# Decay rows in a tile of two units and a tile of four, first weights behind the third chunk's loads: one change to a chunked scan with a feed-forward block

## The chip, the cores and the metric

The kernel runs on one core of one Trainium2 chip. The metric is device microseconds of one execution, from launch to the last store. The kernel before takes 327.71 us, the median of three runs (324.82 to 328.68).

## The reference, cut to what matters

Two stages follow each other. The first is a scan with decay over 768 positions for 4 batches and 8 heads (head width 32, state width 16), done in chunks. The second is a feed-forward block of width 2048 over the 3072 resulting tokens of width 256.

```python
log_a = np.log(np.clip(a, 1e-06, 1.0))
for c in range(nc):                                   # chunk after chunk
    cum = np.cumsum(la, axis=-1)                      # la: this chunk of log_a
    L = np.exp(cum[:, :, :, None] - cum[:, :, None, :]) * causal
    CB = np.einsum('bhin,bhjn->bhij', Cc, Bc)         # scores
    y_intra = np.einsum('bhij,bhjd->bhid', CB * L, xc)
    y_inter = np.einsum('bhin,bhnd->bhid', Cc, state) * np.exp(cum)[:, :, :, None]
    y[:, :, sl] = y_intra + y_inter
    state = decay_full[:, :, None, None] * state + np.sum(Bx, axis=2)
...
h = x @ w_in                                          # x: y as (tokens, 256)
g = np.maximum(0.01 * h, h)
return (g @ w_out).astype(np.float32)
```

## The kernel before, in words

**Units.** A chunk is 96 positions, so there are 8 chunks of 4 batches: 32 units, each with all 8 heads of one batch in one chunk. Unit u belongs to chunk u // 4. For every unit the kernel needs a decay tile `lt` (the exponentials L for the 8 heads, with the decay to the carried state appended), multiplies scores into it and contracts the result with x.

**Two ways to a decay tile.** Units 0 and 1 get theirs from masks alone (`decay_direct`). Units 2 to 15 get theirs from TensorE (`decay_pe`, L245): one product of a left tile `dl` and a right tile `dr` makes the differences of the cumulative sums in PSUM tile `pd`, and ScalarE takes the exponential (L261). The constant rows of `dl` and `dr` are filled once (`fill_pair`, `fill_less`). The rows that depend on the unit come from `parts_d`, the cumulative sums split in three bf16 parts and stored to HBM, by two loads (`decay_rows_of`, L238 into `dr` and L241 into `dl`). Before, there are two `dl`/`dr` pairs with two units each; when the two units of a pair have been used by TensorE, the next two units' rows are loaded into it. Units 16 to 31 take another way (`decay_rows`, `decay_sub`, `decay_exp`: a broadcast load, a subtraction on GpSimd and an exponential), worked off in pairs by `pair_block` between the steps of the feed-forward block.

**The lead.** The loop over u from 0 to 14 (L616) does the first 16 units one after the other. In its round u stand, in this order: the scores of unit u + 1 (TensorE L305, VectorE L310), the decay of unit v = u + 2 (L248, L261), the products of unit u (L322, and L331 for the state to carry), ScalarE's copies out (L353, L358), then loads on the SyncE queue: rows for later decay tiles, `bc` (B and C), `bn` (B again, for the state), `xs` (x) and `raw` (the coded weights of one block f of the hidden width). The state of a unit goes through GpSimd (L356) into the x tile of the same batch one chunk later. `LEAD_PASSES` says in which rounds one or more decode passes run.

**Decoding weights.** Each of the 16 blocks f of the weights comes as 64-bit numbers in two halves and is decoded to a high part `wh` and a low part `wl` of fp32 by five passes on VectorE (hold L412, shift L418, sign L425, low L432, rest L445) and two on ScalarE (`decode_abs` L407 ahead of the five, `decode_high` L438 ahead of rest). `RAWS` is the number of raw tiles; the load of block f + RAWS is issued when the low pass of block f is done.

**The feed-forward block.** 96 steps (t, f): a token tile t of 512 and a block f. Step s runs six matmuls into `hp` (L508: x high with w high, x high with w low, x low with w high, for two halves), an activation on ScalarE, the low half of it on VectorE (L521), and three steps later six matmuls of the second product (L536). The steps start with t = 0, 1, 2 in turn for the first 7 blocks f, and go on with f = 7 to 15 for t = 0, then 1, then 2, and then t = 3, 4, 5. `PAIR` names the step at which the block of each pair of later units stands; its loads, subtraction and exponential stand five, three and two steps ahead. When the last f of a token tile is through, `take` adds the parts (L559) and stores. `late_sums`, at the end of step 24, makes the cumulative sums for units 16 to 31.

The order on every engine is the order in which the program is written: each engine works through its own queue and waits on semaphores. SyncE runs ahead of the others until one of its loads waits for a free buffer.

## Time and profile before

| what | value |
|---|---|
| time, median of three runs | 327.71 us (324.82 to 328.68) |
| the profiled execution's own time | 328.9 us |
| its span, first to last instruction | 327.2 us |
| mean granted TensorE clock | 0.982 |
| TensorE matmul busy | 317.5 us, 97% |
| ScalarE busy | 168.1 us, 51% |
| VectorE busy | 161.0 us, 49% |
| GpSimd busy | 78.0 us, 24% |
| moved by DMA | 27.86 MB |
| first feed-forward matmul starts | 41.02 us |

In the profile PE is TensorE's matmul, PEld its weight load, DVE VectorE, ACT ScalarE, POOL GpSimd and SPq the queue of loads and stores on SyncE. A row of a timeline is: start in us, length in us, engine, line of the kernel, operation, output and inputs with sizes, count, and in brackets the idle time before it with what ended it. The chain of waits is followed back from the last instruction. A row of the table of stretches gives the stretch, its length, the busy time of each engine with the count of instructions, then the granted TensorE clock (1.00 is full speed), the mean busy share of the DMA engines and the rate in GB/s. The profiled execution took 328.9 us, 1.2 us above the median of the timed runs and 1.7 us longer than its own span.

### The profile page before, as it was taken

How to read it: one execution, taken by the hardware profiler on the slowest of the kernel's cores; microseconds unless marked ns; L12 is line 12 of the kernel's file. 1: busy time of each engine (PE TensorE's matmuls, PEld its weight loads, DVE VectorE, ACT ScalarE, POOL GpSimd, SP SyncE). 2: the span in 40 equal slices, each digit the busy share in tenths (PEclk: the TensorE clock that was granted, in tenths of full speed). 3: DMA queues.
4: the chain of work that ended last, by engine and by line, in shares of the span. 5: the costliest groups of instructions: out<-in, count | busy, mean ns of one | idle time of the engine just before them, and what ended most of it. 6: DMA issues, size and time to landing. Idle time of an engine off the chain costs nothing.

```text
span 327.2 us, 6238 instructions
## 1 busy us (share of the span) xinstructions
PE 317.5 (97%) x2425; PEld 251.6 (77%) x2425; DVE 161.0 (49%) x308; ACT 168.1 (51%) x335; POOL 78.0 (24%) x164
## 2 busy tenths in 40 slices
PE   8969999999999999999999999999999999999994
PEld 4546688888887887788688878888878788888883
DVE  7637989888888524352615352425252212322221
ACT  5645768566667353535354535454544433433331
POOL 4735740000000133335434235252410000000000
PEclk9967999999999999999999999999999999999999
DMA  5795413333350560120263054302010000100001
GB/s 174 219 271 182 137 66 128 128 128 130 92 191 0 156 180 0 66 86 0 103 200 86 1 172 132 86 0 87 2 64 0 2 0 2 62 4 0 2 0 65
DMA packets 11527, 27.86 MB, mean 85 GB/s; under 512 B 2313, under 2 KB 2793, under 8 KB 11497
## 3 DMA queue, kind: packets, MB, share of 16 engines
q1 hardware_dynamic: 11353, 27.33, 26.5%
q8 instruction: 19, 0.31, 0.4%
q10 hardware_dynamic: 144, 0.13, 0.1%
q14 instruction: 11, 0.09, 0.1%
HBM read 24.14 MB, written 3.32 MB: 84 GB/s over the span
## 4 chain that ended last, share of the span: by engine, by line
PE 94%; DMA 2%; ACT 1%; DVE 1%; issue 1%; SPq 0%; ACTq 0%; DVEq 0%
PE hp L508 39%; PE py L536 35%; PE sc L536 5%; PE sc L305 2%; PE sc L382 2%; DMA dl<-parts_d 2%; PE sc L322 2%; PE py L322 2%; PE pd L248 2%; PE sc L508 1%; PE sc L109 1%; PE py L331 1%; DVE lt L310 0%; PE sc L331 0%; PE pd L225 0%
## 5 line engine op out<-in xcount | busy, mean ns | idle before, releaser
L521 DVE TENSOR_TENSOR gl<-hp,gh 128x512 fp32r<-128x512 f32 x94 | 65.0, 692 | 141.6 <-ACT hp L518 141.6
L515 ACT ACTIVATE gh<-hp 128x512 fp32r<-128x512 f32 x94 | 56.3, 599 | 111.3 <-PE hp L508 111.2
L508 PE MATMUL hp<-xh,wh 128*128 128x512 f32 x188 | 73.4, 390 | 0.0
L508 PE MATMUL hp<-xl,wh 128*128 128x512 f32 x188 | 73.2, 389 | 0.0
L508 PE MATMUL hp<-xh,wl 128*128 128x512 f32 x188 | 73.1, 389 | 0.0
L536 PE MATMUL py<-gh,wh 128*128 128x512 f32 x164 | 65.3, 398 | 0.7 <-ACT gh L515 0.7
L536 PE MATMUL py<-gh,wl 128*128 128x512 f32 x164 | 63.9, 390 | 0.0
L536 PE MATMUL py<-gl,wh 128*128 128x512 f32 x164 | 63.9, 389 | 0.0
L518 ACT ACTIVATE hp<-hp 128x512 f32<-128x512 f32 x94 | 55.7, 593 | 0.0
L508 PEld LDWEIGHTS hp<-xl,wh 128*128 128x128 f32 x188 | 35.3, 188 | 7.4
L508 PEld LDWEIGHTS hp<-xh,wh 128*128 128x128 f32 x188 | 35.3, 188 | 7.4
L508 PEld LDWEIGHTS hp<-xh,wl 128*128 128x128 f32 x188 | 35.3, 188 | 7.3
L271 POOL TENSOR_TENSOR lt<-lt,ccol 112x768 f32<-112x768 f32 x16 | 23.5, 1470 | 69.8 <-DMA lt<-crow_d 68.1
L356 POOL COPY xs<-stage 16x64 f32<-16x64 f32 x112 | 28.4, 254 | 45.7 <-ACT stage L353 25.6
L536 PEld LDWEIGHTS py<-gh,wh 128*128 128x128 f32 x164 | 30.8, 188 | 9.9 <-issue 2.0
L536 PEld LDWEIGHTS py<-gl,wh 128*128 128x128 f32 x164 | 30.8, 188 | 6.5
L536 PEld LDWEIGHTS py<-gh,wl 128*128 128x128 f32 x164 | 30.8, 188 | 6.0
L280 POOL TENSOR_SCALAR_AFFINE_SELECT lt<-lt 96x768 f32<-96x768 f32 x16 | 14.0, 877 | 41.0 <-ACT lt L279 41.0
L310 DVE TENSOR_TENSOR lt<-sc,lt 112x384 f32<-112x384 f32 x32 | 16.3, 551 | 11.1 <-PE sc L305 7.4
L261 ACT ACTIVATE lt<-pd 112x768 f32<-112x768 f32 x15 | 12.2, 811 | 12.5 <-PE pd L248 6.7
L391 DVE TENSOR_TENSOR lt<-sc,lt 112x384 f32<-112x384 f32 x32 | 15.6, 550 | 0.5
L279 ACT ACTIVATE lt<-lt 112x768 f32<-112x768 f32 x16 | 13.4, 840 | 4.2 <-POOL lt L271 4.2
(101 smaller groups left out, 292.7 us busy)
## 6 DMA issues: line engine op xcount, KB each, us to landing
raw<-w_l SPq DMA_DIRECT2D x16, 512.0 KB
lt<-crow_d SPq DMA_DIRECT2D x16, 336.0 KB
bc<-bc_l SPq DMA_DIRECT2D x8, 608.0 KB
xs<-x_l SPq DMA_DIRECT2D x16, 192.0 KB
out_l<-ob SPq DMA_DIRECT2D x11, 256.0 KB
bn<-bn_l SPq DMA_DIRECT2D x8, 231.0 KB
out_l<-obh ACTq DMA_DIRECT2D x1, 128.0 KB
out_l<-obh SPq DMA_DIRECT2D x1, 128.0 KB
```

The source lines that it names most:

```text
L271: nc.gpsimd.tensor_tensor(out=lts[u], in0=lts[u], in1=ccol[:, u * NH:(u + 1) * NH].unsqueeze(2).to_broadcast([QE, NH, Q]), op=ALU.subtract,)
L279: nc.scalar.activation(lt, lt, AF.Exp)
L280: nc.gpsimd.affine_select(out=lt[:Q], in_=lt[:Q], pattern=[[0, NH], [1, Q]], compare_op=ALU.is_ge, fill=0.0, base=0, channel_multiplier=-1,)
L310: nc.vector.tensor_tensor(out=heads, in0=sc[:QE, :, :2 * Q], in1=heads, op=ALU.mult)
L322: nc.tensor.matmul(space[hh * D:(hh + 1) * D, g, off:off + Q], lhsT=xs[:kk, h * D:(h + 1) * D], rhs=mt[:kk, h, :], start=True, stop=True,)
L356: nc.gpsimd.tensor_copy(to[:, :, hh], stage[hh * D:hh * D + N])
L391: nc.vector.tensor_tensor(out=heads, in0=spaces[half][:QE, :, 2 * Q * e:2 * Q * (e + 1)], in1=heads, op=ALU.mult,)
L508: nc.tensor.matmul(hp, lhsT=w_half[half][:, f, k * 128:(k + 1) * 128], rhs=x[t][:, k, :], start=(n == 0), stop=(n == 5),)
L515: nc.scalar.activation(ghs[s], hp, AF.Prelu, alpha=0.01)
L518: nc.scalar.activation(hps[s], hps[s], AF.Prelu, alpha=0.01)
L521: nc.vector.tensor_tensor(out=gls[s], in0=hps.pop(s), in1=ghs[s], op=ALU.subtract)
L536: nc.tensor.matmul(op, lhsT=w_half[half][:, f, DM + m * 128:DM + (m + 1) * 128], rhs=x, start=(first and i == 0), stop=(last and i == 2),)
```

## The change

The two `dl`/`dr` pairs of two units each become one for two units and one for four (`ROWS = (2, 4)`). The first holds units 2 and 3, then 8 and 9, then 14 and 15; the second holds units 4 to 7, then 10 to 13. Units 2 to 7 are loaded ahead of the lead. The rows for units 8 and 9 are loaded in round 1, where those for 6 and 7 stood; for units 10 to 13 in round 5, for 14 and 15 in round 7. The constant rows `less` of the tile of four are copied by VectorE (four copies), where GpSimd copied two before. The first weights are no longer loaded ahead of the lead but in round 3, behind `bc` and `bn` of the third chunk; blocks 1 and 2 follow in rounds 8 and 10, block 3 after the low pass of block 0 (`RAWS` 3 in place of 4). The x of the fourth chunk is loaded in round 5 in place of 3. `decode_abs` of block 0 stands in round 7 in place of 4, and the seven passes of the lead in rounds 9 to 14 in place of 5 to 13. Four pairs of later units stand one to three steps earlier (`PAIR`: 30, 34, 38, 44 in place of 31, 36, 41, 46).

In the changed kernel the lines from L105 on have numbers higher by 1 to 7: L248 is L252, L310 is L314, L238 is L242.

```diff
@@ -32,19 +32,20 @@
 LAG = 3
 WARM = 4
 WARM2 = 1
-RAWS = 4
+RAWS = 3
 
 TURNS, SHARED = 3, 7
 
 DIRECT = 2
 PE_DECAY = 16
-SLOTS = 4
-
-PAIR = {16: 31, 18: 36, 20: 41, 22: 46, 24: 52, 26: 57, 28: 62, 30: 68}
+
+ROWS = (2, 4)
+
+PAIR = {16: 30, 18: 34, 20: 38, 22: 44, 24: 52, 26: 57, 28: 62, 30: 68}
 LAST_OUT = 74
 
 
-LEAD_PASSES = (5, 6, 8, 9, 11, 12, 13)
+LEAD_PASSES = (9, 10, 11, 12, 13, 14, 14)
 PASSES = (2, 2) + (3,) * 19 + (2,) * 3 + (3,) * 7
 KD = Q + 3 * NH + 3
 MAG_MIN = float(np.uint32(0x38000000).view(np.float32))
@@ -127,9 +128,8 @@
     after = const.tile([Q, QE], F32, name="after")
     later = const.tile([Q, Q], BF16, name="later")
     less = const.tile([128, NH], BF16, name="less")
-
-    dls = [const.tile([128, 2, QE], BF16, name=f"dl{i}") for i in range(SLOTS // 2)]
-    drs = [const.tile([128, 2, NH, Q], BF16, name=f"dr{i}") for i in range(SLOTS // 2)]
+    dls = [const.tile([128, n, QE], BF16, name=f"dl{n}") for n in ROWS]
+    drs = [const.tile([128, n, NH, Q], BF16, name=f"dr{n}") for n in ROWS]
     reach = [const.tile([Q, NH, Q], F32, name=f"reach{i}") for i in range(DIRECT)]
     nc.vector.memset(upto, 0.0)
     nc.vector.memset(upto[:, :Q], 1.0)
@@ -163,18 +163,19 @@
 
 
 
-    def fill_pair(i):
+    def fill_later(i):
+        n = ROWS[i]
         nc.vector.memset(dls[i][Q:], 1.0)
         nc.vector.memset(dls[i][Q:Q + 3 * NH, :, Q:], 0.0)
-        nc.vector.tensor_copy(dls[i][:Q], upto_b.unsqueeze(1).to_broadcast([Q, 2, QE]))
+        nc.vector.tensor_copy(dls[i][:Q], upto_b.unsqueeze(1).to_broadcast([Q, n, QE]))
         nc.vector.tensor_copy(
             drs[i][:Q].rearrange("p b h i -> p (b h) i"),
-            later.unsqueeze(1).to_broadcast([Q, 2 * NH, Q]),
-        )
-
-    def fill_less(b, copy):
+            later.unsqueeze(1).to_broadcast([Q, n * NH, Q]),
+        )
+
+    def fill_less(i, b, copy):
         rows = slice(Q, Q + 3 * NH)
-        copy(drs[b // 2][rows, b % 2], less[rows].unsqueeze(2).to_broadcast([3 * NH, NH, Q]))
+        copy(drs[i][rows, b], less[rows].unsqueeze(2).to_broadcast([3 * NH, NH, Q]))
 
     def fill_reach(u):
         nc.gpsimd.affine_select(
@@ -228,13 +229,16 @@
             )
 
     def slot_of(u):
-        return divmod((u - DIRECT) % SLOTS, 2)
+        b = (u - DIRECT) % sum(ROWS)
+        return (1, b - ROWS[0]) if b >= ROWS[0] else (0, b)
 
     def decay_rows_of(u):
 
-        p, (i, _) = u * NH, slot_of(u)
-        r = Q + 3 * NH
-        rows = parts_d[p:p + 2 * NH]
+        i, b = slot_of(u)
+        assert b == 0
+        n = ROWS[i]
+        p, r = u * NH, Q + 3 * NH
+        rows = parts_d[p:p + n * NH]
         nc.sync.dma_start(
             drs[i][r:r + 3].rearrange("i b h q -> i (b h) q"), rows.rearrange("p i q -> i p q")
         )
@@ -585,32 +589,31 @@
             out=la, in0=la, scalar1=1e-6, scalar2=1.0, op0=ALU.max, op1=ALU.min,
         )
         nc.scalar.activation(la, la, AF.Ln)
-        fill_pair(0)
+        fill_later(0)
         pds = [[out_tile(), out_tile()], decay_tile()]
         for u in range(DIRECT):
             fill_reach(u)
         for u in range(DIRECT):
             decay_mask(pds[u])
         split_sums(first[:, 0, :Q])
-        fill_less(0, nc.scalar.copy)
-        fill_less(1, nc.scalar.copy)
+        for b in range(ROWS[0]):
+            fill_less(0, b, nc.scalar.copy)
         second = score_tile()
         keep_warm(second[:, 1], WARM2)
         columns(erev, after, AF.Exp, second[:, 0])
-        fill_pair(1)
+        fill_later(1)
         nc.sync.dma_start(parts_d, parts)
         decay_direct(0, pds[0])
         decay_of(0, pds[0])
-        for u in range(DIRECT, DIRECT + SLOTS, 2):
-            decay_rows_of(u)
+        decay_rows_of(DIRECT)
+        decay_rows_of(DIRECT + ROWS[0])
         fetch_bc(1)
         fetch_bn(1)
         fetch_x(1)
-        fetch_w(0)
         scores(0)
         state_decay(0)
-        for b in range(2, SLOTS):
-            fill_less(b, nc.gpsimd.tensor_copy)
+        for b in range(ROWS[1]):
+            fill_less(1, b, nc.vector.tensor_copy)
         decay_direct(1, pds[1])
         decay_of(1, pds[1])
         for u in range(PE_DECAY - 1):
@@ -624,13 +627,15 @@
             rests.append(unit_out(u, unit_tile()))
             if u == 0:
                 decay_pe(v, decay_tile())
-            if v % 2 and v + SLOTS <= PE_DECAY:
-                decay_rows_of(v + SLOTS - 1)
+
+
+            i, b = slot_of(v)
+            new = v + sum(ROWS) + 1 - ROWS[i]
+            if b == ROWS[i] - 1 and new < PE_DECAY:
+                decay_rows_of(new)
             if u:
                 rests.popleft()()
             settle()
-            if u == 4:
-                decode_abs(0)
 
 
             if u in (2, 6):
@@ -640,13 +645,15 @@
                 state_decay(3)
             if u == 1:
                 fetch_x(2)
-            if u == 3:
+            if u == 5:
                 alloc_x(3)
                 fetch_x(3)
             if u in (3, 7):
                 fetch_bn(u // 4 + 2)
-            if u in (4, 8, 9):
-                fetch_w({4: 1, 8: 2, 9: 3}[u])
+            if u in (3, 8, 10):
+                fetch_w({3: 0, 8: 1, 10: 2}[u])
+            if u == 7:
+                decode_abs(0)
             decode(LEAD_PASSES.count(u))
         rests.popleft()()
         settle()
```

SyncE's queue in the lead, from the store of the cumulative sums (L601 and L605) on. A load into `dl` or `dr` shows the units it brings in its size: 3x16x96 and 24x2x96 are two units, 3x32x96 and 24x4x96 four. Before:

```order
L238 DMA dr_121<-parts_d 3x16x96
L241 DMA dl_119<-parts_d 24x2x96
L238 DMA dr_122<-parts_d 3x16x96
L241 DMA dl_120<-parts_d 24x2x96
L85 DMA bc<-bc_l 128x1216
L89 DMA bn<-bn_l 112x528
L99 DMA xs<-x_l 96x512 x2
L81 DMA raw<-w_l 128x1024
L238 DMA dr_121<-parts_d 3x16x96
L241 DMA dl_119<-parts_d 24x2x96
L99 DMA xs<-x_l 96x512 x2
L85 DMA bc<-bc_l 128x1216
```

And the same queue of the changed kernel, from the load of the tile of four on:

```order
L242 DMA dr_122<-parts_d 3x32x96
L245 DMA dl_120<-parts_d 24x4x96
L86 DMA bc<-bc_l 128x1216
L90 DMA bn<-bn_l 112x528
L100 DMA xs<-x_l 96x512 x2
L242 DMA dr_121<-parts_d 3x16x96
L245 DMA dl_119<-parts_d 24x2x96
L100 DMA xs<-x_l 96x512 x2
L86 DMA bc<-bc_l 128x1216
L90 DMA bn<-bn_l 112x528
L82 DMA raw<-w_l 128x1024
L242 DMA dr_122<-parts_d 3x32x96
```

The first rows that are loaded during the lead stood behind one chunk's loads and the first weights and belonged to units 6 and 7. Now the first such rows belong to units 8 and 9 and stand behind one chunk's loads; the rows for units 10 to 13 stand behind the loads of two chunks and the first weights.

VectorE around the first scores, before (L170 is the last of the fills, L310 multiplies the scores of units 0, 1, 2 into their decay tiles, two instructions for a unit):

```order
L167 MEMSET dl_120 32x224
L168 MEMSET dl_120 24x2x8
L169 COPY dl_120<-upto_b 96x224
L170 COPY dr_122<-later 96x1536
L310 TENSOR_TENSOR lt<-sc,lt 112x384 x6
```

And in the changed kernel:

```order
L168 MEMSET dl_120 32x448
L169 MEMSET dl_120 24x4x8
L170 COPY dl_120<-upto_b 96x448
L171 COPY dr_122<-later 96x3072
L314 TENSOR_TENSOR lt<-sc,lt 112x384 x2
L178 COPY dr_122<-less 24x768 x4
L314 TENSOR_TENSOR lt<-sc,lt 112x384 x4
```

The fills have twice the size, and four copies of `less` now stand between the scores of unit 0 and those of unit 1.

VectorE in the last rounds of the lead, in the changed kernel (L429, L436, L449, L416 and L422 are the passes sign, low and rest of block 0 and hold and shift of block 1):

```order
L429 SCALAR_TENSOR_TENSOR w_551<-raw,w_551 128x512
L314 TENSOR_TENSOR lt<-sc,lt 112x384 x2
L365 TENSOR_TENSOR xl<-py,xh 128x2x96
L436 SCALAR_TENSOR_TENSOR w_551<-raw,w_551 128x512
L314 TENSOR_TENSOR lt<-sc,lt 112x384 x2
L365 TENSOR_TENSOR xl<-py,xh 128x2x96
L449 TENSOR_TENSOR wl<-w_551,wh 128x512
L314 TENSOR_TENSOR lt<-sc,lt 112x384 x2
L365 TENSOR_TENSOR xl<-py,xh 128x2x96
L416 TENSOR_SCALAR w_757<-w_757 128x512
L422 TENSOR_SCALAR w_757<-w_757 128x512
```

Before, the rest pass stood two units earlier:

```order
L445 TENSOR_TENSOR wl<-w_424,wh 128x512
L310 TENSOR_TENSOR lt<-sc,lt 112x384 x2
L361 TENSOR_TENSOR xl<-py,xh 128x2x96
L412 TENSOR_SCALAR w_638<-w_638 128x512
L310 TENSOR_TENSOR lt<-sc,lt 112x384 x2
L361 TENSOR_TENSOR xl<-py,xh 128x2x96
L418 TENSOR_SCALAR w_638<-w_638 128x512
L310 TENSOR_TENSOR lt<-sc,lt 112x384 x2
```

The last multiplication of the lead's scores, for unit 15, now stands directly behind the rest pass of block 0; two of them stood between that pass and unit 15's before.

## The prediction

> **What bounds the kernel now.** I read the page first, then the chain of waits from the start to 46 us, TensorE's timeline there, the table of stretches for the clock and the loads, and last VectorE's, ScalarE's and GpSimd's timelines. The page says that TensorE is the bound, and its clock row that one place differs (slices 3 and 4 of 40, about 16 to 33 us):

> ```profile
> PE 317.5 (97%) x2425; PEld 251.6 (77%) x2425; DVE 161.0 (49%) x308; ACT 168.1 (51%) x335; POOL 78.0 (24%) x164
> PEclk9967999999999999999999999999999999999999
> PE 94%; DMA 2%; ACT 1%; DVE 1%; issue 1%; SPq 0%; ACTq 0%; DVEq 0%
> ```

> So time is won only where TensorE stands still or runs at a low clock. In the chain of waits (start, length, what) that is one place, the load of the rows for unit 6:

> ```profile
> 12.27 6.81 DMA dl<-parts_d
> 19.12 0.89 PE pd L248 x2
> ```

> The load is issued at 12.27 us and lands at 19.08. TensorE's timeline shows the round times of the lead: the decay of units 3 to 7, then 10 to 15, and the first feed-forward matmul.

> ```profile
> 10.39 0.38 PE L109 MATMUL sc<-idle 128*128 128x512 bf16 x1
> 11.45 0.48 PE L248 MATMUL pd<-dr,dl 123*112 123x384 bf16 x2 [0.15 <-ACT lt L261]
> 13.02 0.53 PE L248 MATMUL pd<-dr,dl 123*112 123x384 bf16 x2
> 14.74 0.53 PE L248 MATMUL pd<-dr,dl 123*112 123x384 bf16 x2
> 19.12 0.89 PE L248 MATMUL pd<-dr,dl 123*112 123x384 bf16 x2 [2.69 <-DMA dl<-parts_d]
> 21.88 0.89 PE L248 MATMUL pd<-dr,dl 123*112 123x384 bf16 x2
> 29.50 0.53 PE L248 MATMUL pd<-dr,dl 123*112 123x384 bf16 x2
> 31.26 0.53 PE L248 MATMUL pd<-dr,dl 123*112 123x384 bf16 x2
> 33.05 0.53 PE L248 MATMUL pd<-dr,dl 123*112 123x384 bf16 x2
> 34.85 0.53 PE L248 MATMUL pd<-dr,dl 123*112 123x384 bf16 x2
> 36.43 0.53 PE L248 MATMUL pd<-dr,dl 123*112 123x384 bf16 x2
> 38.85 0.53 PE L248 MATMUL pd<-dr,dl 123*112 123x384 bf16 x2
> 41.02 0.50 PE L508 MATMUL hp<-xh,wh 128*128 128x512 f32 x1
> ```

> A round takes 1.57 and 1.72 us early on, and 1.76, 1.79, 1.80 and 1.58 from unit 10 to 14. Units 6 to 10 take 10.38 us for four rounds, where four at 1.75 are 7.0. The same two products take 0.89 us at 19.12 and 0.53 at 29.50. The stretches tell why (clock, DMA share and GB/s are the last three):

> ```profile
> 10.00:15.00 5.00, 4.84 (x109) 3.03 (x97) 3.46 (x9) 3.50 (x9) 2.83 (x11) 1.00 0.91 271
> 15.00:20.00 5.00, 2.31 (x48) 1.20 (x50) 2.34 (x6) 1.13 (x3) 2.53 (x8) 0.84 1.01 295
> 20.00:25.00 5.00, 5.00 (x84) 3.29 (x84) 1.80 (x5) 3.22 (x8) 1.63 (x7) 0.50 0.85 235
> 18.00:19.00 1.00, 0.00 (x0) 0.00 (x0) 0.00 (x0) 0.00 (x0) 0.00 (x0) 0.68 1.02 286
> 28.00:29.00 1.00, 1.00 (x37) 0.74 (x36) 0.86 (x3) 0.67 (x1) 0.92 (x2) 0.70 0.08 26
> ```

> The clock goes from 1.00 to 0.50 within 18 to 19 us, during the wait, and back within 28 to 29 us. So the late load costs 2.69 us of standing still and about 3.4 us (10.38 - 7.0) of slow rounds. [...] Here a wait of 2.69 us was enough, and the low clock lasted some 10 us with TensorE busy from 19.12 on; the measurement decides. [...]

> **The change, part by part.** The sum goes against the profiled execution, 328.9 us (span 327.2 and 1.7 around it). It lies 1.2 above the median; a run without the slow rounds would be near 325.5 by these rows, and the lowest of the three timed runs, 324.82, looks like one. I take the profiled scale for the changed kernel, without a correction, since it should hardly wait there.

> *The rows for units 6 and 7 come early.* They are in the tile of four, loaded ahead of the lead: the wait of 2.69 us goes, and with it the reason for the low clock. What is late next are the rows for units 10 to 13. How late, the sizes of the queue tell (KB each):

> ```profile
> raw<-w_l SPq DMA_DIRECT2D x16, 512.0 KB
> bc<-bc_l SPq DMA_DIRECT2D x8, 608.0 KB
> xs<-x_l SPq DMA_DIRECT2D x16, 192.0 KB
> bn<-bn_l SPq DMA_DIRECT2D x8, 231.0 KB
> ```

> Before, `bc`, `bn`, two `xs` and the first weights lie ahead of unit 6's rows: 608 + 231 + 384 + 512 = 1735 KB, 1.78 MB. At the mean of 271 and 295 GB/s, counted from 10 us, that takes until 16.3; the rows landed at 19.08, 2.8 us behind the mean rate. Now units 10 to 13 have those 1735 KB and 384 + 608 + 231 more ahead, 2958 KB or 3.03 MB: 2.83 MB are through by 20 us, the rest at 235 GB/s by 20.85, and with the same 2.8 us the rows land at 23.65. The tile of four doubles the small pieces of its own loads, for which I add 0 to 0.7 us: 23.6 to 24.4. Units 8 and 9 have 1223 KB ahead, less than the 1735 KB that landed at 19.08, and are wanted at 12.2 + 5 x 1.70 = 20.7: no wait.

> *VectorE's fills.* They stand ahead of the first scores, and four copies now stand behind those of unit 0:

> ```profile
> 6.13 0.24 DVE L167 MEMSET dl<- 32x224 bf16 x1
> 6.66 0.55 DVE L170 COPY dr<-later 96x1536 bf16<-96x1536 bf16 x1
> 7.39 1.02 DVE L310 TENSOR_TENSOR lt<-sc,lt 112x384 f32<-112x384 f32 x2 [0.18 <-PE sc L305]
> 9.63 1.02 DVE L310 TENSOR_TENSOR lt<-sc,lt 112x384 f32<-112x384 f32 x2 [1.22 <-ACT lt L261]
> 8.97 1.60 POOL L177 COPY dr<-less 24x768 bf16<-24x768 bf16 x2
> ```

> The larger fills take about 0.24 + 0.40 us more, of which 0.18 was idle: unit 0's scores are multiplied from 7.9 to 8.9 in place of 7.4 to 8.4. No row has a VectorE copy of `less`, which reads each element 96 times over. Half of L170's 0.55 us is the lower bound, 0.28 each; GpSimd's 0.8 each is the upper one. I take VectorE's own row with one step down, its 0.55 for half the elements, that is 0.47 each one behind the other (as a pair of L310 takes 1.02): 1.9 us, to 10.8. [...] Unit 1's multiplication so runs from 10.8, not 9.63, and frees the score tiles at 11.3 and 11.8. The warm-up matmul of the next round, at 10.39 before, needs the first and waits 0.9 us; unit 3's decay comes at 12.2 in place of 11.45: **0.75 us lost** (0.2 with copies of 0.28, 2.2 with 0.8). GpSimd loses its two copies, on no path.

> *The rounds.* From 12.2, seven rounds of 1.70 us (no pass on VectorE, between 1.57 and 1.80) bring unit 10's decay to 24.1. Its rows land between 23.6 and 24.4: **0.2 us lost**, 24.3. Then five rounds with a pass at 1.75: unit 15's decay at 33.05, in place of 38.85. ScalarE's `decode_abs` of block 0 wants the weights that lie just ahead of those rows, so it adds no wait of its own.

> *The end of the lead.* The rest pass, with ScalarE's copy ahead of it, now stands in round 13:

> ```profile
> 34.80 0.62 ACT L438 CAST wh<-w 128x512 fp32r<-128x512 f32 x1
> 40.26 0.32 ACT L358 CAST xh<-py 128x192 fp32r<-128x192 f32 x1
> 36.08 1.28 DVE L445 TENSOR_TENSOR wl<-w,wh 128x512 fp32r<-128x512 f32 x1
> 45.39 0.69 DVE L445 TENSOR_TENSOR wl<-w,wh 128x512 fp32r<-128x512 f32 x1
> ```

> In that round ScalarE's last cast ended at 40.58, 1.73 us after unit 15's decay at 38.85. `wh` now follows with 0.62 (2.35), then `wl` with 0.69 to 1.28 (3.0 to 3.6). The first feed-forward matmul comes 2.17 us after the decay, and the second, 0.33 later, reads `wl`: it waits 0.5 to 1.1 us, **0.7 us lost**. The pass with 1.28 us stretched a round to 2.42 us before (36.43 to 38.85); that excess is gone with the move, since from unit 10 on I counted 1.75 throughout. The lead ends at 33.05 + 2.17 + 0.7 = 35.9 in effect, against 41.02: **5.1 us won**.

> *The later units.* The pair of units 20 and 21 stood at step 41, where token tile 1 also ends:

> ```profile
> 157.89 1.95 DVE L391 TENSOR_TENSOR lt<-sc,lt 112x384 f32<-112x384 f32 x4
> 160.68 1.28 DVE L559 TENSOR_TENSOR ob<-py,ob 128x512 f32<-128x512 f32 x2
> 161.50 0.47 PE L536 MATMUL py<-gh,wh 128*128 128x512 f32 x1 [0.75 <-ACT gh L515]
> ```

> L559 stands behind the pair's work on VectorE, and TensorE wants the PSUM tile that it frees; the first of the two ends near 161.3, just ahead of the matmul. At step 38 the pair is out of that way: **0.75 us won** (0 if the named activation was the cause). The new spacing of four steps leaves the loads for units 20 and 21 one step less (2.72 us) between the release of their tiles and their exponential; ScalarE may wait about 1 us there, which the three steps between a first and its second product cover.

> *The rest at nothing:* the other passes move within VectorE's idle time of the lead; raw tiles, three in place of four, leave about three steps from a load's issue to its use, 8 us for 512 KB, some 2 us at the rates above. If that cover were gone, one step would wait for a load, 1 to 2 us.

> Sum: 5.1 + 0.75 = 5.85; 328.9 - 5.85 = 323.05. **Forecast 323.0 us**, 1.4% under the median. Its own range is 322.0 to 324.2, from the bounds of the copies, of the rows' landing and of `wl`.

> **The rivals.**

> *The copies run at GpSimd's pace.* 0.8 us each: unit 3's decay comes 2.2 us late, not 0.75; the rows' 0.2 us are then hidden. 323.05 + 1.45 - 0.2 = 324.3. For it speaks that no VectorE row repeats elements, against it that L170 moves 1536 elements in 0.55 us. Chance 0.13.

> *All the new costs are hidden.* Copies at the lower bound (0.55 us less), rows in time (0.2), `wl` in time (0.7): 321.6, and 321.0 with the lead's rounds at 1.65. Chance 0.14.

> *The wait only moves, to unit 10, and the clock falls again.* This is the slow side. Its place is the decay of unit 10, its price the wait and the low clock. If the rows land at 27, 3 us late, TensorE stands still as long as it did before; then the last five rounds run at the 2.76 us that lie between 19.12 and 21.88. The low clock lasted about 10.2 us, of which a share of 1 - 1.75/2.76 is lost, 3.7 us: 323.05 + 2.8 + 3.7 = 329.6, slower than before. It decides from a wait of some 2 us, as the 0.15 us ahead of unit 3 did nothing and 2.69 us did. For it speaks that these rows lie behind 1.7 times as many bytes, against it that the rates above land them at 24.4 at the latest. Chance 0.08.

> *The low clock is not the wait's doing.* It then falls all the same: the 3.4 us stay, 326.4. For it speaks nothing in the rows, against it the stretch of 18 to 19 us, where the clock falls with TensorE idle. Chance 0.07. [...]

> **How the numbers follow.** The forecast keeps 0.58. The predicted time is its 323.0. The range 321.0 to 326.6 takes in the second, third and fifth case and leaves out the slow one and the tails. Two per cent, about what a measurement of this kernel can tell from no change, is 6.55 us: 321.16 or less is faster, 334.3 or more slower. Only the far end of the third case and a profiled scale that lies 1.2 us too high reach the first: 0.15. No case reaches 334.3; 0.02 for what I don't see. Within 2%: 0.83.

> **What would show it.** Right: the clock row reads 9 throughout the lead; the chain names no `dl` load of 6 us; unit 3's decay is at 12.2, unit 10's at 24.3, unit 15's at 33, the first feed-forward matmul near 35.3, with a wait for L449 behind it; L178 takes about 0.55 us on VectorE; no wait of 0.75 us in the step where token tile 1 ends. Wrong: a wait of over 2 us ahead of unit 10's decay and a clock of 0.50 behind it, copies of 0.8 us, or waits for weights or for units 16 and 20 after 36 us.

## The result, and the profile after

The changed kernel takes **323.88 us** (median of 20 executions, 323.24 to 328.15); the kernel before, timed beside it on the same chip, 325.8 us (20 executions, 324.82 to 328.71). The ratio is **0.9939 [0.9917, 0.9961]**: 0.6% less time, which is inside the 2% band. The profiled execution took 323.83 us (span 322.1). The ratios in this part leave out executions that lie over 1.5% above the fastest of their kernel; the medians and the ranges count all.

The page of the changed kernel, its busy row, its clock row and its chain, beside the rows of before:

```profile
PE 315.7 (98%) x2425; PEld 250.4 (78%) x2425; DVE 163.7 (51%) x312; ACT 167.4 (52%) x335; POOL 75.5 (23%) x162
PEclk9999999999999999999999999999999999999999
PE 92%; DVE 3%; ACT 2%; issue 1%; ACTq 0%
```

The two slices of low clock are gone, and the chain holds no load any more. The stretches of the lead (clock, DMA share and GB/s last) say the same:

```profile
15.00:20.00 5.00, 5.00 (x128) 3.37 (x126) 3.90 (x10) 3.39 (x9) 3.79 (x14) 1.00 0.87 279
20.00:25.00 5.00, 5.00 (x128) 3.27 (x126) 3.71 (x10) 3.65 (x11) 3.44 (x12) 1.00 0.83 231
```

TensorE is busy through the stretch in which it stood still before. Its timeline, with the decays of units 2 and 3, then 9 to 15, and the first two feed-forward matmuls:

```profile
11.05 0.53 PE L252 MATMUL pd<-dr,dl 123*112 123x384 bf16 x2
12.10 0.38 PE L110 MATMUL sc<-idle 128*128 128x512 bf16 x1 [0.51 <-DVE lt L314]
13.07 0.53 PE L252 MATMUL pd<-dr,dl 123*112 123x384 bf16 x2
23.09 0.53 PE L252 MATMUL pd<-dr,dl 123*112 123x384 bf16 x2
24.71 0.53 PE L252 MATMUL pd<-dr,dl 123*112 123x384 bf16 x2
26.85 0.53 PE L252 MATMUL pd<-dr,dl 123*112 123x384 bf16 x2
28.43 0.53 PE L252 MATMUL pd<-dr,dl 123*112 123x384 bf16 x2
30.19 0.53 PE L252 MATMUL pd<-dr,dl 123*112 123x384 bf16 x2
31.77 0.53 PE L252 MATMUL pd<-dr,dl 123*112 123x384 bf16 x2
33.35 1.04 PE L309 MATMUL sc<-bc 32*112 32x192 f32 x8 [0.45 <-DVE lt L314]
34.32 0.53 PE L252 MATMUL pd<-dr,dl 123*112 123x384 bf16 x2
36.72 0.50 PE L512 MATMUL hp<-xh,wh 128*128 128x512 f32 x1
37.35 0.50 PE L512 MATMUL hp<-xh,wl 128*128 128x512 f32 x1
```

No decay waits for rows. Three rounds are longer than the rest: the one to unit 3 (2.02 us), the one from unit 10 to 11 (2.14) and the one from unit 14 to 15 (2.55). The first and the last have a VectorE row beside them, and the last also a GpSimd row:

```profile
9.48 1.97 DVE L178 COPY dr<-less 24x768 bf16<-24x768 bf16 x4
31.45 1.37 DVE L429 SCALAR_TENSOR_TENSOR w<-raw,w 128x512 uint32<-128x512 uint32 x1
36.61 0.69 DVE L449 TENSOR_TENSOR wl<-w,wh 128x512 fp32r<-128x512 f32 x1 [0.79 <-ACT wh L442]
```

```profile
31.22 1.05 POOL L290 TENSOR_TENSOR bn<-bn,erev 112x512 f32<-112x512 f32 x1
```

A reader who wants the gain by stage takes two marks, the start of unit 0's decay (L225 before, L226 now) and the first feed-forward matmul (L508, L512). Before, these are 7.21 and 41.02 us: a lead of 33.81, and 286.2 us from there to the end of the span. After, 8.24 and 36.72: 28.48, and 285.4. So the lead gave 5.3 us and the rest 0.8, while this execution's first decay came 1.03 us later; the span is 5.1 us shorter. Against the profile of before that kept its clock (7.66 and 36.89 us, a lead of 29.23; the first run below) the lead gives 0.8 us, and in a second profile of the changed kernel, with a lead of 29.10, only 0.1; the rest gives 0.8 there too.

**What the time before was made of.** Three executions had been shown of the kernel before. With all those taken beside the runs below there are 94 whose mean clock is known. One window of 3.41 us at half clock (the shortest low stretch in a profile, in the run with one weight block more ahead of the rows, below) takes 0.005 off the mean over some 325 us, so an execution below 0.996 is counted as one that had at least one.

| kernel | executions | median us | ratio to before [95%] | with a mean clock below 0.996 |
|---|---|---|---|---|
| before | 94 | 326.2 | | 58 |
| changed | 20 | 323.88 | 0.9939 [0.9917, 0.9961] | 1 |
| changed, again | 12 | 324.58 | 0.9926 [0.9901, 0.995] | 0 |

The 36 executions of before that kept the clock have a median of 325.4 us, the 58 others 327.2, and the fifteen with the lowest mean (under 0.985) 328.9. The profiled one, with three windows (10.24 us) at half clock, was of that last kind, and of the three shown times two, 327.71 and 328.68, lie where executions with a low clock do, and one, 324.82, with the clean ones. The change takes away the low clock, which is most of the gain over such an execution and nothing over a clean one; over a clean one its medians are 0.8 to 1.5 us lower, of which 0.8 is won behind the lead.

### The profile page after: what moved, and what is told of

The parts are those of the page before. It is cut to its first block, busy times and chain, and to the rows that moved or that the text cites. A ratio compares the mean times of both kernels' runs of the same rounds, so it can differ in the third digit from the quotient of the medians.

```text
span 322.1 us, 6238 instructions
## 1 busy us (share of the span) xinstructions
PE 315.7 (98%) x2425; PEld 250.4 (78%) x2425; DVE 163.7 (51%) x312; ACT 167.4 (52%) x335; POOL 75.5 (23%) x162
## 3 DMA queue, kind: packets, MB, share of 16 engines
HBM read 24.14 MB, written 3.32 MB: 85 GB/s over the span
## 4 chain that ended last, share of the span: by engine, by line
PE 92%; DVE 3%; ACT 2%; issue 1%; ACTq 0%
PE hp L512 39%; PE py L540 35%; PE sc L540 5%; PE sc L386 2%; PE sc L326 2%; PE sc L309 2%; DVE lt L314 1%; PE pd L252 1%; PE py L326 1%; PE sc L512 1%; PE sc L110 1%; ACT lt L265 1%; PE py L226 1%; DVE dr L178 1%; PE sc L198 0%
## 5 line engine op out<-in xcount | busy, mean ns | idle before, releaser
L519 ACT ACTIVATE gh<-hp 128x512 fp32r<-128x512 f32 x94 | 56.1, 597 | 109.8 <-PE hp L512 109.8
L512 PE MATMUL hp<-xh,wl 128*128 128x512 f32 x188 | 73.3, 390 | 0.1
L512 PE MATMUL hp<-xh,wh 128*128 128x512 f32 x188 | 73.4, 390 | 0.0
L512 PE MATMUL hp<-xl,wh 128*128 128x512 f32 x188 | 73.2, 389 | 0.0
L512 PEld LDWEIGHTS hp<-xh,wl 128*128 128x128 f32 x188 | 35.3, 188 | 7.8 <-DVE wl L449 0.5
L512 PEld LDWEIGHTS hp<-xl,wh 128*128 128x128 f32 x188 | 35.3, 188 | 7.3
L512 PEld LDWEIGHTS hp<-xh,wh 128*128 128x128 f32 x188 | 35.3, 188 | 7.3
L360 POOL COPY xs<-stage 16x64 f32<-16x64 f32 x112 | 27.7, 247 | 44.3 <-ACT stage L357 28.6
L314 DVE TENSOR_TENSOR lt<-sc,lt 112x384 f32<-112x384 f32 x32 | 16.3, 552 | 4.6 <-PE sc L309 2.0
## 6 DMA issues: line engine op xcount, KB each, us to landing
raw<-w_l SPq DMA_DIRECT2D x16, 512.0 KB, 4.7
bc<-bc_l SPq DMA_DIRECT2D x8, 608.0 KB
xs<-x_l SPq DMA_DIRECT2D x16, 192.0 KB, 5.4
bn<-bn_l SPq DMA_DIRECT2D x8, 231.0 KB, 4.9
```

The costliest lines, as they stand in the source:

```text
L314: nc.vector.tensor_tensor(out=heads, in0=sc[:QE, :, :2 * Q], in1=heads, op=ALU.mult)
L360: nc.gpsimd.tensor_copy(to[:, :, hh], stage[hh * D:hh * D + N])
L512: nc.tensor.matmul(hp, lhsT=w_half[half][:, f, k * 128:(k + 1) * 128], rhs=x[t][:, k, :], start=(n == 0), stop=(n == 5),)
L519: nc.scalar.activation(ghs[s], hp, AF.Prelu, alpha=0.01)
```

## The experiments

All theories here are about three questions: what makes the rows late, what makes the clock fall, and what the new costs are. "Theory one" is the prediction's account, unless the text says otherwise.

### The kernel before once more

No edit.

> The kernel before, unchanged. Theory one (the late rows cost every run the wait, but only some runs the low clock): the wait ahead of unit 6's decay is there again with 2 to 3 us; most runs lie at 325 to 326.5 us with a mean clock of 1.00, and the few at 327.5 or more have a clock near 0.98. Theory two (the wait always brings the low clock): every run shows a clock near 0.98, and the spread of the times has another cause.

Measured: 326.14 us (324.8 to 329.73), ratio 0.9997 [0.9961, 1.0033]; 6 of 12 executions with a low clock, the profiled one (324.8 us) without. TensorE's timeline in that one, units 6 and 8:

```profile
18.01 0.53 PE L248 MATMUL pd<-dr,dl 123*112 123x384 bf16 x2 [1.14 <-DVE lt L310]
22.22 0.53 PE L248 MATMUL pd<-dr,dl 123*112 123x384 bf16 x2 [0.80 <-DMA dl<-parts_d]
```

The rows are late here too, twice, by 1.9 us in all, each time by less than the 2 to 3 us expected of unit 6. (The view names VectorE for unit 6's wait, but the load landed at 17.97 us, just ahead of the product's 18.01.) The two products take 0.53 us behind each wait: the clock stayed up. So the wait is a property of the kernel, and its length varies from execution to execution; in these two profiles the low clock came with the long one.

### The pairs of later units at their old steps

```diff
-PAIR = {16: 30, 18: 34, 20: 38, 22: 44, 24: 52, 26: 57, 28: 62, 30: 68}
+PAIR = {16: 31, 18: 36, 20: 41, 22: 46, 24: 52, 26: 57, 28: 62, 30: 68}
```

> The changed kernel with the later pairs at their old steps (31, 36, 41, 46). Theory one (pair 20 held up TensorE in the step where token tile 1 ends): a wait of about 0.75 us comes back there, and the time is 0.75 above the changed kernel's 323.9, so 324.6. Theory two (that wait was a coincidence of the one profile): no such wait, 323.9.

Measured: 325.16 us (324.23 to 329.69), ratio 0.9968 [0.9947, 0.9989]; 1 of 12 with a low clock, and by chance the profiled one is that one. Two rows of TensorE's timeline, the first in the middle of unit 7's products:

```profile
25.67 0.38 PE L326 MATMUL py<-lt,xs 112*32 112x96 f32 x3 [2.21 <-issue]
```

```profile
162.73 0.47 PE L540 MATMUL py<-gh,wh 128*128 128x512 f32 x1 [0.75 <-ACT gh L519]
```

The second row is the wait of before, back with its 0.75 us; from the first feed-forward matmul to the end it is 286.2 us again. So the term is shown in place and size, though four pairs went back together and not the one of units 20 and 21 alone. The median, 325.16 us where 324.6 was expected, lies 1.1 us above the two relatives timed beside it on the same chip (324.04 and 324.05, below), and at the 325.2 of the clean executions of before there: over a clean execution the pairs' move is nearly all that the median gains.

What TensorE waits for is not told by that row: it names the activation L519, which ended at 162.68, and the first L563 had ended at 162.58. In the changed kernel the same place reads:

```profile
156.08 1.28 DVE L563 TENSOR_TENSOR ob<-py,ob 128x512 f32<-128x512 f32 x2
156.91 0.47 PE L540 MATMUL py<-gh,wh 128*128 128x512 f32 x1
157.07 0.60 ACT L519 ACTIVATE gh<-hp 128x512 fp32r<-128x512 f32 x1 [0.88 <-PE hp L512]
```

There the matmul starts before the activation and behind the first of the two L563 (done near 156.76), so the tile that L563 frees is what it needs, as the prediction had it.

The first row was not expected: a stop of 2.21 us that no semaphore explains, and the clock is 0.50 for the three windows of 3.41 us behind it. It is taken up below.

### The four copies of `less` on GpSimd

```diff
-            fill_less(1, b, nc.vector.tensor_copy)
+            fill_less(1, b, nc.gpsimd.tensor_copy)
```

> The changed kernel with the four copies of less on GpSimd in place of VectorE. Theory one (the 1.97 us of copies hold up unit 1's scores): the wait of 0.51 us ahead of the warm-up matmul of round 1 is gone and the lead is 0.5 us shorter, 323.4. Theory two (GpSimd's 3.3 us for them make the state copies or unit 4's decay late): a wait of 0.5 us or more ahead of unit 4 or 5, 323.9 or more.

Measured: 324.04 us (323.22 to 324.94), ratio 0.9948 [0.9928, 0.9968]. TensorE's timeline, units 2 and 3 and the middle of unit 7's products:

```profile
11.09 0.53 PE L252 MATMUL pd<-dr,dl 123*112 123x384 bf16 x2
12.53 0.48 PE L252 MATMUL pd<-dr,dl 123*112 123x384 bf16 x2 [0.16 <-ACT lt L265]
23.77 0.28 PE L326 MATMUL py<-lt,xs 112*32 112x96 f32 x3 [0.29 <-issue]
```

The round to unit 3 takes 1.44 us in place of 2.02: the copies on VectorE cost 0.58 us there, and the wait for L314 is gone with them. In the median that can't be seen: it is 324.04 us where 323.4 was expected. And the stop without a semaphore is here again, 0.29 us, ahead of the same group of three matmuls.

### The tile of four alone, the weights as before

```diff
-LEAD_PASSES = (9, 10, 11, 12, 13, 14, 14)
+LEAD_PASSES = (5, 6, 8, 9, 11, 12, 13)
...
         fetch_x(1)
+        fetch_w(0)
...
-            if u in (3, 8, 10):
-                fetch_w({3: 0, 8: 1, 10: 2}[u])
-            if u == 7:
+            if u in (4, 8):
+                fetch_w({4: 1, 8: 2}[u])
+            if u == 4:
                 decode_abs(0)
```

> The changed kernel with the first weights loaded ahead of the lead, and decode_abs and the passes of the lead in the rounds where they stood before; the tiles of two and four stay. Theory one (the tile of four is what took the wait away; the place of the first weights is of little weight): no wait for rows of 0.5 us or more, the wait for wl at the first feed-forward step is gone, 323.3. Theory two (the weights ahead of the second and third chunk's loads bring a wait for those): a wait of 1 us or more for rows, bc or bn in rounds 4 to 8, 325.

Measured: 324.05 us (323.34 to 326.05), ratio 0.9943 [0.9911, 0.9975]; 2 of 12 with a low clock. Its profile has no wait for rows. Four units loaded at once are therefore enough to take the wait away in most executions, wherever the first weights stand. That their move adds a margin, which two of the twelve lacked, is likely but not shown: it is two of 12 here against one of 32 with the move. The wait for `wl` is gone as expected (the first two feed-forward matmuls start 0.34 us apart, 0.63 in the changed kernel), but the median of 323.3 us that this was to give did not come.

### The weights' move alone, with two tiles of two

```diff
-        fetch_w(0)
...
-            if u == 4:
-                decode_abs(0)
...
-            if u in (4, 8, 9):
-                fetch_w({4: 1, 8: 2, 9: 3}[u])
+            if u in (3, 8, 10, 11):
+                fetch_w({3: 0, 8: 1, 10: 2, 11: 3}[u])
+            if u == 7:
+                decode_abs(0)
...
-LEAD_PASSES = (5, 6, 8, 9, 11, 12, 13)
+LEAD_PASSES = (9, 10, 11, 12, 13, 14, 14)
```

The edits are to the kernel before.

> The kernel before with one part of the change: the first weights behind the third chunk's loads, with the first absolute value and the passes as late as in the changed kernel; tiles of two and two, the pairs of units at their old steps. Theory one, the bytes ahead of unit 6's rows set its wait: 1223 KB in place of 1735 KB, 1.8 to 2.2 us earlier, so the waits of 1.14 and 2.69 us seen so far at unit 6 shrink to 0 to 0.7, the low clock does not come, and the median is 324.7 to 325.3 us (0.75 us of the token tile's end still in it). Theory two, the wait comes from there being only four units of rows, loaded as a tile is released: waits of about 1 us stay at unit 6 or move to unit 8, some executions fall to the low clock, and the median stays at 325.8 to 326.2.

Measured: 325.55 us (323.97 to 329.16), ratio 0.9949 [0.9916, 0.9981]; 3 of 12 with a low clock, where the kernel before had 20 of 29 on the same chip. In its profile unit 6 no longer waits, but unit 10 does:

```profile
24.83 0.53 PE L248 MATMUL pd<-dr,dl 123*112 123x384 bf16 x2 [1.00 <-DMA dl<-parts_d]
```

Both theories hold a part, and the median lies between theirs: fewer bytes ahead took the wait from unit 6, and with rows for only four units in the tiles a later load comes late. That the next large block in the queue is what makes it late is argued, not shown.

### One and two weight blocks more ahead of the rows of units 10 to 13

```diff
+            if u == 5:
+                fetch_w(1)
             i, b = slot_of(v)
...
-            if u in (3, 8, 10):
-                fetch_w({3: 0, 8: 1, 10: 2}[u])
+            if u in (3, 10):
+                fetch_w({3: 0, 10: 2}[u])
```

> The changed kernel with one 512 KB weight block more ahead of the rows of units 10 to 13 in SP's queue (it is the second block, which otherwise comes three rounds later). Theory one, the rows land when the bytes ahead of them are through: in the changed kernel they landed at 24.2 us, 0.5 us ahead of unit 10's decay at 24.71; 0.524 MB more at 235 to 295 GB/s is 1.8 to 2.2 us, so they land near 26.2 and TensorE waits 1.3 to 1.7 us there. A wait of 1.14 us left the clock at 1.00 in the second profile of the kernel before, so I expect no low clock: 325.0 to 325.5 us median. Theory two, small loads slip past large ones or the rows wait for the release of their tile and not for bytes: no wait over 0.6 us, 324 us.

Measured: 326.09 us (324.9 to 328.02), ratio 0.9979 [0.9946, 1.0013]; 8 of 12 with a low clock. The decay of unit 10, the middle of unit 10's products and the decay of unit 13:

```profile
26.17 0.53 PE L252 MATMUL pd<-dr,dl 123*112 123x384 bf16 x2 [1.52 <-DVE lt L314]
31.61 0.28 PE L326 MATMUL py<-lt,xs 112*32 112x96 f32 x3 [1.12 <-issue]
32.89 0.89 PE L252 MATMUL pd<-dr,dl 123*112 123x384 bf16 x2
```

The wait is 1.52 us where 1.3 to 1.7 was worked out from the bytes (the view names VectorE, which had long been done; the rows landed at 26.13 us, near the 26.2 expected, and that came last). Behind it the clock stayed up; it fell after the second stop, the one without a semaphore. That the median would stay at 325.0 to 325.5 was a miss: I had taken one wait for the whole of the idle time.

The other kernel has the second and the third block there:

```diff
+            if u == 5:
+                fetch_w(1)
+                fetch_w(2)
             i, b = slot_of(v)
...
-            if u in (3, 8, 10):
-                fetch_w({3: 0, 8: 1, 10: 2}[u])
+            if u == 3:
+                fetch_w(0)
```

> The changed kernel with two 512 KB weight blocks more (the second and the third) ahead of the rows of units 10 to 13. Theory one: they land some 4 us later, near 28.2, TensorE waits 3.3 to 3.7 us at unit 10's decay, and the clock is 0.50 behind it, three windows of 3.4 us, in which rounds take about 2.76 in place of 1.7 us: 3.5 + 3.5 to 3.9 us on top of 323.9, 331 us, every execution slow and not only some. Theory two, the low clock is not the wait's doing: 327.4 us with the clock at 1.00. Theory three, bytes ahead do not set the landing: 324 us.

Measured: 328.37 us (324.71 to 331.88), 11 of 12 with a low clock. The ratio is 1.0009 [0.9972, 1.0046]; the median lies 1.3 us above that of the kernel before on the same chip (327.06). The profiled execution was the fastest of the twelve: its rows landed at 26.03 us, where 28.2 was expected, with a wait of 1.31 us and this stretch:

```profile
20.00:25.00 5.00, 4.48 (x116) 2.79 (x106) 3.10 (x9) 3.46 (x11) 3.33 (x11) 1.00 1.04 370
```

370 GB/s, where the other profiles here have 209 to 319 in this stretch: the rate of the loads is not the same from one execution to the next, and with it the landing. The kernel once more, without an edit:

> The kernel with two weight blocks ahead of the rows of units 10 to 13 once more, for a second profile: its first profile was the fastest of twelve executions (324.71 us, loads at 370 GB/s between 20 and 25 us, rows at 26.1), the median was 328.4. Theory one: at a rate of 210 to 280 GB/s in that stretch the rows land at 27 to 28.5 us, TensorE waits 2 to 3.7 us ahead of unit 10's decay, a window of 3.4 us is then idle for more than half, and the clock is 0.50 for one to three such windows: 327 to 331 us. Theory two, the rate does not matter and the slow executions have another cause: a wait of 1.3 us again, with a low clock or without.

Measured: 328.34 us. Units 9 to 12 and the stretches:

```profile
22.61 0.53 PE L252 MATMUL pd<-dr,dl 123*112 123x384 bf16 x2
24.15 0.28 PE L326 MATMUL py<-lt,xs 112*32 112x96 f32 x3 [0.56 <-issue]
27.40 0.89 PE L252 MATMUL pd<-dr,dl 123*112 123x384 bf16 x2 [2.23 <-DMA dl<-parts_d]
30.16 0.89 PE L252 MATMUL pd<-dr,dl 123*112 123x384 bf16 x2
32.91 0.54 PE L252 MATMUL pd<-dr,dl 123*112 123x384 bf16 x2
```

```profile
20.00:25.00 5.00, 4.44 (x124) 2.92 (x112) 3.23 (x9) 3.21 (x10) 3.15 (x10) 1.00 0.95 319
25.00:30.00 5.00, 2.77 (x47) 1.67 (x42) 1.29 (x3) 2.12 (x5) 1.16 (x5) 0.61 1.00 228
```

This is the profile of before at another place: the load of the rows late (27.35 us), TensorE idle for 2.23 us, two windows at half clock with rounds of 2.75 us, and 328.3 us. The bytes ahead of the rows make the wait: the rows landed at 24.23 us in the changed kernel, at 26.13 with one block more ahead and at 27.35 here. In the window before the clock fell (22.72 to 26.14 us) TensorE was idle for 1.53 us, 0.56 of them in the stop and the rest in the wait, so it is the two together that the low clock followed, in this one execution.

### The first three passes one round earlier

```diff
-LEAD_PASSES = (9, 10, 11, 12, 13, 14, 14)
+LEAD_PASSES = (8, 9, 10, 12, 13, 14, 14)
```

> The changed kernel with its first three passes one round earlier (rounds 8, 9 and 10), so that VectorE's sign pass runs ahead of GpSimd's product of 1.05 us and not beside it. Theory one, the sign pass took 1.37 us in place of 0.68 because GpSimd's product ran beside it, and this stretched the round to unit 15's decay to 2.55 us: the pass takes 0.68, no gap of 0.45 us ahead of unit 13's scores, the first feed-forward matmul comes 0.6 to 0.8 us earlier and the median is 323.1 to 323.4 us. Theory two, the round is long for another reason, or what is gained there is lost at the wait for wl: 323.8 to 324.1 us.

Measured: 323.54 us (323.19 to 324.11), ratio 0.988 [0.984, 0.992]. VectorE's sign pass and GpSimd's product, and two rows of TensorE's timeline:

```profile
30.01 0.68 DVE L429 SCALAR_TENSOR_TENSOR w<-raw,w 128x512 uint32<-128x512 uint32 x1
32.41 1.06 POOL L290 TENSOR_TENSOR bn<-bn,erev 112x512 f32<-112x512 f32 x1
```

```profile
25.47 0.53 PE L252 MATMUL pd<-dr,dl 123*112 123x384 bf16 x2 [0.77 <-DMA dl<-parts_d]
30.37 0.28 PE L326 MATMUL py<-lt,xs 112*32 112x96 f32 x3 [0.57 <-issue]
```

The pass takes 0.68 us when GpSimd's product isn't beside it, not 1.37, and no multiplication holds up the last rounds (1.58 us from unit 14 to 15, 2.55 in the changed kernel). But 1.37 us is no fixed price: in twelve of the fourteen profiles of this case a sign or rest pass started beside that product and took 0.86 to 1.38 us, and each ended 0.54 to 0.55 us behind the product's end, however long the two overlapped. So of the 0.68 us that the pass takes alone, at most some 0.14 lay ahead of the product's end, an estimate from these times. VectorE's multiplications with one input in PSUM were not longer beside the same product (two of L314 1.02 us at 33.06 here, as at 34.86 without it; L365 0.35 us at 24.06 in the changed kernel, as at 26.20 without it).

The median lies between the two theories, and the ratio says more than the change gave, since the kernel before had mostly a low clock on this chip (327.06 us). In this profile the gain was eaten by a wait for unit 10's rows, 0.77 us, and by another stop without a semaphore. So the changed kernel's rows stand near the edge: they landed 0.5 us ahead of need in its first profile (the last piece at 24.23, the decay at 24.71), 0.9 ahead in its second (23.20 and 24.14), and 0.77 behind in a relative with the same loads.

### The first weights behind the rows, and the best of all

```diff
             if u == 5:
+                fetch_w(0)
                 alloc_x(3)
...
-            if u in (3, 8, 10):
-                fetch_w({3: 0, 8: 1, 10: 2}[u])
-            if u == 7:
+            if u in (8, 10):
+                fetch_w({8: 1, 10: 2}[u])
+            if u == 8:
                 decode_abs(0)
```

The kernel called best has this, the four copies on GpSimd, and the first three passes one round earlier. Both stood beside the unedited changed kernel, on one chip.

> The changed kernel once more, beside the next two on the same chip: 323.9 us median, the clock at 1.00 in nearly every execution (over 0.996), unit 10's rows landing 0.5 us ahead of its decay or up to 0.8 us behind it. If the rare late executions of the changed kernel have the cause that I see in its relatives (a block of 256 instructions for TensorE that comes late behind the loads), a stop, where this profile has one, stands ahead of the 706th or the 962nd of TensorE's instructions, and nowhere else without a semaphore.

> The changed kernel with the first weight block issued just behind the rows of units 10 to 13 in place of just ahead of them, and its absolute value one round later (the passes stay). Theory one, bytes ahead set the landing: 0.524 MB less, so the rows land 1.8 to 2.2 us earlier, near 22.3 us, and a wait ahead of unit 10's decay (none to 0.8 us in the changed kernel and its relative) is gone in every execution; ScalarE's absolute value no longer delays unit 10's exponential (a round of 2.14 us becomes 1.7). 323.3 to 323.7 us. Theory two, the rows were not late in most executions and the lead ends where the passes end: 323.9 us as before.

> As the run before, and the two other findings together: the four copies of less on GpSimd (unit 3's decay 0.5 us earlier) and the first three passes one round earlier (sign pass 0.68 us and not 1.37, the last rounds 0.6 us shorter). If the three gains add up: 322.3 to 322.8 us. If the round times are set elsewhere (instruction blocks that come late, the weights that then land nearer to their first pass), they don't: 323.5 to 324 us.

| kernel | median us | lowest to highest | ratio to before [95%] |
|---|---|---|---|
| changed, again | 324.58 (12) | 323.17 to 334.67 | 0.9926 [0.9901, 0.995] |
| first weights behind the rows | 323.82 (7) | 323.15 to 324.37 | 0.9916 [0.9885, 0.9948] |
| best | 323.0 (6) | 322.54 to 323.6 | 0.9898 [0.9866, 0.993] |

None of the three had an execution below 0.996 of the clock (the one of 334.67 us had 0.998, and what it spent its time on isn't known). The changed kernel once more was expected at 323.9 us; its profile has neither a wait for rows nor a stop. With the first weights behind the rows there is no wait for rows either: they landed at 21.78 us (22.3 was expected), 2.3 ahead of unit 10's decay. The round from unit 10 to 11 was expected to shrink to 1.7 us when ScalarE's absolute value left it:

```profile
24.06 0.53 PE L252 MATMUL pd<-dr,dl 123*112 123x384 bf16 x2
26.20 0.53 PE L252 MATMUL pd<-dr,dl 123*112 123x384 bf16 x2
29.05 0.28 PE L326 MATMUL py<-lt,xs 112*32 112x96 f32 x3 [0.29 <-issue]
```

It is 2.14 us as before, so that reading was wrong. What lengthens the round can be seen in VectorE's rows, of the changed kernel and of the one with the copies on GpSimd:

```profile
25.26 1.02 DVE L314 TENSOR_TENSOR lt<-sc,lt 112x384 f32<-112x384 f32 x2 [0.85 <-PE pd L252]
```

```profile
26.86 1.02 DVE L314 TENSOR_TENSOR lt<-sc,lt 112x384 f32<-112x384 f32 x2 [0.69 <-ACT xh L362]
```

The first is the multiplication of unit 9's scores. Both of its inputs were done by 24.78 us, and it starts only at 25.26, 0.45 us after the semaphore instruction just ahead of it; in most other rounds of the lead that distance is 0.04. It frees the tile of the scores late, so the next scores are late (L309's eight matmuls take 1.05 us from 25.87, 0.63 the round before), and with them unit 11's decay. In the records it is VectorE's 64th instruction, and in ten of the fourteen profiles the 64th is such a multiplication with such a delay (0.44 to 0.46 us). The second row is unit 10's: in that kernel and in the one with the weights' move alone VectorE has four instructions fewer ahead, the 64th falls one unit later, and so does the long round (unit 11 to 12 takes 1.98 and 2.16 us there, unit 10 to 11 only 1.76 and 1.58). Where TensorE waited for rows at unit 10 anyway, the delay did not lengthen the round (1.58 us from unit 10 to 11 with one and with two blocks ahead and with the passes one round earlier). Why that instruction starts late, no run here shows.

Best's timeline shows unit 3's decay early, one wait, and the first feed-forward matmul:

```profile
11.87 0.48 PE L252 MATMUL pd<-dr,dl 123*112 123x384 bf16 x2 [0.16 <-ACT lt L265]
26.84 1.05 PE L309 MATMUL sc<-bc 32*112 32x192 f32 x8 [0.53 <-DVE lt L314]
35.13 0.51 PE L512 MATMUL hp<-xh,wh 128*128 128x512 f32 x1
```

From unit 0's decay (7.63) to the first feed-forward matmul it is 27.50 us, against 28.48 and 29.10 in the two profiles of the changed kernel. Its median is 1.6 us under that of the changed kernel on the same chip, and 0.9 under the one of the other; 322.3 to 322.8 us was expected if the three findings add up, so that most of them did, but not all: the 0.53 us ahead of unit 11's scores are new: VectorE's hold pass now waits for ScalarE's absolute value of the weights (1.01 us, to 25.90), and the multiplication that frees a score tile is queued behind it.

## Why the prediction was right, point by point

The forecast was 323.0 us with a range of 321.0 to 326.6; the median is 323.88. "Within 2%" is what came.

- **The wait and the low clock: right.** No row wait in the changed kernel's two profiles, the clock at 1.00 in the lead, 1 low execution of 32 against 58 of 94. The lead is 5.3 us shorter from mark to mark, where 5.1 was worked out; in the second profile it is 4.7.
- **"A run without the slow rounds would be near 325.5": right**, 325.4 in the median of 36. What this meant for the gain wasn't drawn out: the shown median of 327.71 us was itself of the kind with a low clock, so 323 is not 1.4% less than the kernel before but 0.6 to 0.7%.
- **The copies: right in size.** 1.97 us for four, 0.49 each (0.47 taken). Counted from unit 0's decay, unit 3's comes 0.59 us later than before in one profile (13.07 - 8.24 against 11.45 - 7.21) and 1.14 in the other; 0.75 was the term.
- **Seven rounds of 1.70: right.** 13.07 to 24.71 is 1.66 each.
- **Unit 10's rows: right.** Forecast to land at 23.6 to 24.4, they landed at 24.23. The wait of 0.2 us did not show, since this execution began its decays 1.03 us later and unit 10's came at 24.71, not 24.3; in a relative it was 0.77.
- **"From unit 10 on I counted 1.75 throughout": wrong.** Five rounds took 9.61 us, not 8.75. The excess of the old rest pass, which had run beside GpSimd's product (1.28 us from 36.08, the product from 35.75 to 36.81), was taken out, but not asked was what the other passes would collide with at their new rounds. The sign pass came to stand beside GpSimd's product for the last chunk (L290) and took 1.37 us in place of 0.68: the last round is 2.55 us. The run with that pass one round earlier shows it. The other long round, 2.14 us, is that of VectorE's late 64th instruction.
- **The wait for `wl`: right in size.** 0.7 us was taken, with 0.5 to 1.1 as its range. `wl` was done 2.98 us after unit 15's decay, as worked out (3.0 to 3.6). TensorE's own rows show little idle time there (37.22 to 37.35 us), but the second feed-forward matmul comes 3.03 us after unit 15's decay (37.35 - 34.32), where it came 2.50 before (41.35 - 38.85). That is 0.53 us lost: 0.30 at `wl` (the first two matmuls start 0.63 us apart, 0.33 before) and 0.23 ahead of them, which the prediction did not have.
- **The pair of units 20 and 21: right.** 0.8 us less after the lead, 0.8 back with the pairs at their old steps, and the row of 0.75 us with them.
- **The sum: partly luck.** 5.3 and 0.8 us are 6.1, where 5.85 was worked out. Counted from unit 0's decay, unit 10's came 0.62 us earlier than forecast (16.47 us, not 17.09), and the five rounds behind it took 0.86 more: two errors that nearly cancel. The profiled time is 0.8 above the sum (323.83 against 323.05) because this execution's first decay came 1.03 us later, which no step of the prediction speaks of; it varies by as much between executions (7.0 to 8.3 us in the changed kernels here).
- **The rivals.** Copies at GpSimd's pace are ruled out (0.49 us each), and so is a clock that falls all the same (1 execution of 32), though the low clock came behind a stop of another kind too, 2.21 us in the profile with the pairs at their old steps. That all new costs are hidden did not come either: the copies cost 0.59 us and the end of the lead 0.53. The slow side, a wait moved to unit 10 with the clock falling again, is a real mechanism that the changed kernel escapes by 0.5 and 0.9 us in its two profiles: with 1 MB more ahead it came, at 328.4 us where that rival had 329.6.

## What to carry to other kernels

Here a late small load in a queue of large ones cost its own wait, 2.69 us in the profile before, and some 3.4 us of slow rounds behind it when TensorE's clock fell; both were decided by margins of some tenths of a microsecond (rows 0.5 and 0.9 us ahead of need in two profiles of the changed kernel, 0.77 behind in a relative), so the same kernel showed several times. Before an edit is priced, ask for each shown time whether the low clock is in it: the mean clock told it here, 0.982 in the profiled execution before and 0.998 in the one after. And when steps are moved to hide them better, look up what other engine works at their new place, not only whether their own engine is free there: the sign pass took 1.37 us beside GpSimd's product and 0.68 away from it.

## What was not expected of the hardware

**TensorE stopped in the lead at one of two instructions, 256 apart.** The stops "<-issue" in the lead, 0.29 to 2.21 us, stand in seven of the fourteen profiles, each at one of two places. Counted in the records, these are TensorE's 706th and 962nd instruction. The page has a queue of 19 packets and 0.31 MB named "instruction", 16 KB each; TensorE has 4913 instructions, 19 times 256 and a rest. So I take a packet to bring a block of 256, an estimate from these counts. The packets in the records, beside the stop:

| profile | packet starts, lasts | first instruction of the block at | idle ahead of it |
|---|---|---|---|
| changed | 21.07, 1.04 | 706th at 23.75 | none |
| copies on GpSimd | 21.00, 1.05 | 706th at 23.77 | 0.29 |
| two blocks ahead | 21.21, 1.09 | 706th at 23.75 | 0.29 |
| two blocks ahead, again | 21.69, 1.02 | 706th at 24.15 | 0.56 |
| pairs at old steps | 23.32, 1.12 | 706th at 25.67 | 2.21 |
| first weights behind the rows | 26.50, 0.89 | 962nd at 29.05 | 0.29 |
| first three passes earlier | 27.50, 1.35 | 962nd at 30.37 | 0.57 |
| one block ahead | 28.87, 1.31 | 962nd at 31.61 | 1.12 |

In each stop the block runs 1.2 to 1.7 us after its packet ended. In the changed kernel the packet started 2.4 us after the block before had begun (the 450th instruction, at 18.68); with the pairs at their old steps, 5.2 us after (18.08). In best, with no large load just ahead, it was 1.1 us (17.43 to 18.55). In the lead 256 instructions last some 5 us (18.68 to 23.75 in the changed kernel), so a packet that starts some 2.5 us after the block before is just in time, an estimate from these 5.07 us, the packet's 1.04 and the 1.2 to 1.7 behind it. The longest stop was 2.21 us, and the clock fell to 0.50 with it. No run changed these packets alone, so that a late one makes the stop, and that it is late because it stands behind the loads, is argued from these times and not shown apart.
